# An opening in halves of 256 queries, silu on GpSimd, 14 warm matmuls, and first LayerNorms moved to other steps, in a fused attention and MLP kernel

## The chip, the cores and the metric

The kernel runs on one core of a Trainium2 chip. The metric is the device time in microseconds; quoted times are medians of several executions. Every execution also leaves the span of the core (from the first to the last instruction, some 1.8 us shorter than the time) and the mean clock that the tensor engine was granted. The engines are called PE (tensor engine; PEld is its weight load), DVE (VectorE), ACT (ScalarE), POOL (GpSimd) and SP (SyncE, which issues DMAs).

## The reference

One block of a diffusion transformer: 2048 tokens of width 512, modulated LayerNorm, attention of 32 query heads over 8 cached key/value heads (the last 512 positions), output projection, second modulated LayerNorm, MLP with ReLU.

```python
mod = (_silu(c) @ w_mod).reshape(c.shape[0], 6, 1, -1)
sa, ca, ga, sb, cb, gb = (mod[:, i].copy() for i in range(6))      # shortened
h = _layernorm(x, axis=-1) * (1 + ca) + sa
x = x + ga * _A_ref(h, A_k_cache, A_v_cache, A_wq, A_wo)           # attention, times wo
h = _layernorm(x, axis=-1) * (1 + cb) + sb
x = x + gb * _B_ref(h, B_w1, B_w2)                                 # relu MLP
```

## The kernel before

The queries are worked in 4 blocks of 512; a block has 32 steps, one for each head. In a step PE computes queries for two heads ahead, scores, the product with v, and in most steps four matmuls of the output projection; ACT does the exponentials, DVE divides by the row sum (o). The LayerNorms and modulations are tasks put at chosen steps. First there is an opening, in which the first LayerNorm, the transposes and the modulation of block 0 are done while the weights arrive. `warm(n)` issues n matmuls of 512 columns of ones whose result nobody reads; they are there to get the PE clock up (in the profile of before the first seven start 0.42 us apart, the nine after them 0.22).

```python
    warm(7)
    silu_exp(5)                     # transpose c on PE, exponential on ACT
    warm(9)
    ...                             # statistics of tile 3 on ACT
    ln_stat(0); ln_stat(1); rstd_add(0, 2); rstd_pow(0, 2)      # four lines in the kernel
    ln_stat(2); rstd_add(2, 3); rstd_pow(2, 4)
    silu_mul(5)                     # three small operations on DVE
    for tl in range(3):
        ln_norm(tl)
    ...                             # tile 3 on ACT
    fs = mod_cols_mm(0, QBK)        # 32 matmuls of one column: modulation of block 0
    for f in fs[:len(fs) // 2]:
        f()
    ln_tposes(0, [0, 2])
    for f in fs[len(fs) // 2:]:
        f()
    mod_cols_evac(0, QBK)
    for tl in range(1, TPB):
        ln_tposes(tl, [0, 2])
        warm(tl)
    ln_mod_ps([0, 2], hT[0], R_hT[0], 1)     # hT: two pieces of 512 on DVE, two on ACT
    ...
    q_mms(0)
    q_mms(1, 5)
```

Both LayerNorms of all blocks use one buffer `xn` (normalised) and one `xnT` (its transpose by DMA):

```python
    def ln_dmaT():
        dma(xnT[...], xn[...], "xnT", reads=R_xn, writes=[R_xnT], transpose=True)    # shortened
    ...
    for b in range(1, NB):
        add(H * b - 20, lambda b=b: load_x(b))
        add_ln(b, 1, H * b - 15)             # 11 steps: 4 statistics, rstd, norm, transpose, modulation
    for b in range(NB - 1):
        add_ln(b, 2, H * (b + 1) + 19)
```

So the first LayerNorm of block 2 begins at step 49 and the second of block 0 at step 51.

## Time and profile before

| | before |
|---|---|
| median | 563.0 us of 3 runs; 562.9 of 6 |
| span | 561.0 us |
| PE busy | 550.8 us, 98% |
| first score matmul | 13.40 us |
| step, without and with the output projection | 2.63 and 3.50 us |
| uneven steps | two groups of four, 14.64 and 14.66 us in place of 13.99 |

A kernel whose PE is busy for 98% can only win where PE does nothing that counts. The views that show these places are in the prediction.

### The profile page before, as it was taken

To read this page: it belongs to the slowest core of one execution; us is meant where nothing else is said; L and a number is where in the kernel's file an instruction comes from. 1 tells how busy PE (TensorE), PEld (TensorE's weight loads), DVE (VectorE), ACT (ScalarE), POOL (GpSimd) and SP (SyncE) were. 2 spreads that over 40 slices of the span, in tenths; PEclk is the share of its full clock that TensorE was granted. 3 is DMA by queue.
4 is the path that set the end of the run, shared out by engine and by line. 5 is a ranking of instruction groups with operands and counts; after the bars stand their busy time and mean duration, and the time that the engine had idled before them with its cause. 6 is when DMAs were issued, how large, how long until landed. Compare 5 with 4: busy or idle time off the path is not lost.

```text
span 561.0 us, 9655 instructions
## 1 busy us (share of the span) xinstructions
PE 550.8 (98%) x4057; PEld 314.7 (56%) x4132; DVE 252.4 (45%) x550; ACT 350.4 (62%) x453; POOL 51.7 (9%) x46
## 2 busy tenths in 40 slices
PE   7999999999999999999999999999999999999998
PEld 3565555555555555555555555555555654444444
DVE  3455556643336745333347453333354448321134
ACT  5986666666666666666666666666666644432500
POOL 1020002003220000033000000332000000000000
PEclk9999999999999999999999999999999999999999
DMA  9797566512132155242532531121214210210001
GB/s 270 205 206 176 143 164 88 113 39 38 39 76 39 39 90 136 56 96 57 132 57 57 85 63 39 39 38 39 39 39 72 44 30 0 40 37 23 21 29 47
DMA packets 113308, 42.66 MB, mean 76 GB/s; under 512 B 93928, under 2 KB 112104, under 8 KB 113256
## 3 DMA queue, kind: packets, MB, share of 16 engines
q1 hardware_dynamic: 112024, 40.82, 34.5%
q10 hardware_dynamic: 1232, 1.15, 0.6%
q8 instruction: 33, 0.54, 0.4%
q14 instruction: 19, 0.16, 0.1%
HBM read 18.35 MB, written 2.10 MB: 36 GB/s over the span
## 4 chain that ended last, share of the span: by engine, by line
PE 93%; DMA 4%; DVE 2%; issue 1%; DVEq 0%
PE psS L1367 27%; PE psO L1367 26%; PE psQ L1367 22%; PE psW L1367 18%; DMA xnT<-xn 3%; DMA x<-in_A_x_dram 1%; DVE o L1512 0%; DVE st L1377 0%; DVE xn L1388 0%; PE psS L1370 0%; DVE acc L1534 0%; DVE mv L1378 0%; DVE hT L1396 0%; DVE rinv L1511 0%; DVE rstd L1593 0%
## 5 line engine op out<-in xcount | busy, mean ns | idle before, releaser
L1501 ACT ACTIVATE PT<-psS 128x1024 bf16<-128x1024 f32 x256 | 262.7, 1028 | 128.2 <-PE psS L1367 128.2
L1367 PE MATMUL psS<-qT,kT 128*128 128x512 bf16 x510 | 151.4, 379 | 0.1
L1367 PEld LDWEIGHTS psO<-v,PT 128*128 128x128 bf16 x2048 | 126.3, 98 | 31.9 <-DVE o L1512 2.6
L1367 PE MATMUL psO<-v,PT 128*128 128x129 bf16 x2048 | 137.0, 220 | 0.6 <-DVE o L1512 0.6
L1367 PE MATMUL psQ<-hT,wq 128*128 128x512 bf16 x505 | 130.2, 379 | 0.2
L1367 PE MATMUL psW<-wo,oT 128*128 128x512 bf16 x452 | 118.1, 379 | 3.2
L1511 DVE RECIPROCAL rinv<-psO 128x4 f32<-128x4 f32 x128 | 23.3, 182 | 216.0 <-PE psO L1367 216.0
L1512 DVE TENSOR_TENSOR o<-psO,rinv 128x512 bf16<-128x512 f32 x128 | 88.5, 691 | 4.7 <-DVE rinv L1511 0.3
L1367 PEld LDWEIGHTS psQ<-hT,wq 128*128 128x128 bf16 x508 | 49.6, 98 | 60.7 <-issue 0.5
L1367 PEld LDWEIGHTS psS<-qT,kT 128*128 128x128 bf16 x512 | 49.5, 98 | 58.9 <-ACT PT L1501 0.7
L1493 ACT ACTIVATE qT<-psQ 128x512 bf16<-128x512 f32 x127 | 75.3, 593 | 0.5 <-PE psQ L1367 0.5
L1680 ACT ACTIVATE wq<-psS 128x512 bf16<-128x512 f32 x56 | 33.4, 597 | 49.4 <-PE psS L1367 49.4
L1367 PEld LDWEIGHTS psW<-wo,oT 128*128 128x128 bf16 x512 | 44.9, 98 | 32.9 <-DVE acc L1534 1.2
L1534 DVE TENSOR_TENSOR acc<-psW,acc 128x512 f32<-128x512 f32 x48 | 33.1, 690 | 6.7 <-PE psW L1367 6.7
L1367 PE MATMUL psO<-wmw,wq 128*128 128x512 bf16 (+1 forms) x164 | 32.7, 352 | 0.3
L1537 POOL TENSOR_TENSOR acc<-acc,gaf 128x512 f32<-128x512 f32 x12 | 15.2, 1266 | 156.5 <-DVE acc L1534 149.7
L1383 POOL TENSOR_TENSOR rstd<-rstd,cst 128x4 f32<-128x4 f32 x7 | 7.2, 1033 | 213.5 <-DVE rstd L1382 213.5
L1691 DVE TENSOR_TENSOR PT<-psO,gbf 128x512 f32<-128x512 f32 (+1 forms) x12 | 7.5, 624 | 40.4 <-PE psO L1367 40.4
L1367 PE MATMUL psS<-h2T,wmw 128*128 128x512 bf16 x110 | 25.2, 379 | 0.1
L1367 PEld LDWEIGHTS psO<-wmw,wq 128*128 128x128 bf16 x168 | 15.3, 98 | 16.6
L1367 PE MATMUL psS<-hT,wmw 128*128 128x512 bf16 x110 | 24.4, 379 | 0.1
L1377 DVE BATCH_NORM_STATS2 st<-x 128x6 f32<-128x512 bf16 x31 | 21.0, 678 | 4.7 <-DMA x<-in_A_x_dram 4.7
(77 smaller groups left out, 189.4 us busy)
## 6 DMA issues: line engine op xcount, KB each, us to landing
wo<-in_A_wo_dram SPq DMA_DIRECT2D x4, 1024.0 KB, 6.0
wq<-in_A_wq_dram SPq DMA_DIRECT2D x7, 512.0 KB, 5.7
wmw<-in_B_w_dram SPq DMA_DIRECT2D x14, 256.0 KB, 3.1
wmw<-in_w_mod_dram SPq DMA_DIRECT2D x5, 512.0 KB, 4.8
oT<-o SPq DMA_TRANSPOSE x128, 2.4
out_dram<-PT SPq DMA_DIRECT2D x15, 128.0 KB, 1.7
x<-in_A_x_dram SPq DMA_DIRECT2D x3, 512.0 KB, 4.2
v<-in_A_v_cache_dram SPq DMA_DIRECT2D x8, 128.0 KB, 4.2
```

What stands on the lines that cost most here:

```text
L1367: kb.op(PE, lambda e: e.matmul(out_ap, lhsT, rhs, start=start, stop=stop), reads=reads, group_writes=[R_b[k] for k in bk], signal=signal)
L1377: kb.op(DVE, lambda e: e.bn_stats(st[:, t, :], x_sb[:, t, :]), reads=[R_x[t]], writes=[R_st[t]])
L1383: kb.op(POOL, lambda e: e.tensor_tensor(rstd[:, sl], rstd[:, sl], cst[:, 0:1].to_broadcast([P, hi - lo]), op=ALU.pow), reads=R_rstd[sl] + ...
L1493: kb.op(ACT, lambda e: e.activation(qT[u % NQT][:, :], bank[bk], ACTF.Copy), reads=[R_b[bk]], writes=[R_qT[u % NQT]])
L1501: kb.op(ACT, lambda e: e.activation(PT[u % NPT][:, pr * 2:pr * 2 + 2, :], s_ps[pr][:, :, :], ACTF.Exp, scale=scale), reads=[R_b[pr * 2], R ...
L1511: kb.op(DVE, lambda e: e.reciprocal(rinv[:, u, :], o_ps[:, :, P]), reads=[R_b[5], R_b[6]], writes=[R_rinv])
L1512: kb.op(DVE, lambda e: e.tensor_tensor(o_sb[u % NOS][:, :, :], o_ps[:, :, 0:P], rinv[:, u, :].unsqueeze(2).to_broadcast([P, TPB, P]), op=A ...
L1534: kb.op(DVE, lambda e: e.tensor_tensor(acc[:, tl, :], bank[WBK], acc[:, tl, :], op=ALU.add), reads=[R_b[WBK], R_acc[tl]], writes=[R_acc[tl]])
L1537: kb.op(eng, lambda e: e.tensor_tensor(acc[:, tl, :], acc[:, tl, :], gaf[:, :], op=ALU.mult), reads=[R_acc[tl], R_ga], writes=[R_acc[tl]])
L1680: kb.op(ACT, lambda e: e.activation(h1T[b % 2][:, fc, :], bank[bk], ACTF.Relu), reads=[R_b[bk]], writes=[R_h1[b % 2][fc]], pre=all_events( ...
L1691: kb.op(DVE, lambda e: e.tensor_tensor(yt[i][:, c0:c1], bank[bk][:, c0:c1], gbf[:, c0:c1], op=ALU.mult), reads=[R_b[bk], R_gb], writes=[R_ ...
```

## The change

The intent is to begin the attention sooner and to keep the two LayerNorms of different blocks out of each other's way. Its core (cut):

```diff
-    warm(7)
+    warm(8)
     silu_exp(5)
-    warm(9)
+    warm(5)
...
+    silu_mul()                      # now three operations on POOL, before the statistics
     ln_stat(0)
...
-    silu_mul(5)
...
-    kb.op(ACT, lambda e: e.activation(xn[:, t3, :], ..., ACTF.Identity, scale=rstd..., bias=s3...)
+    kb.op(POOL, lambda e: e.tensor_scalar(xn[:, t3, :], x_sb[:, t3, :], s3..., rstd..., op0=ALU.add, op1=ALU.mult)
...
+    ln_tposes(0, TB[0])
+    ln_tposes(1, TB[0])
+    mod_half(0, 0, DVE)             # 256 columns
+    ln_norm(2)
+    mod_half(0, 2, ACT)
+    mod_half(0, 1, DVE)
+    mod_half(0, 3, ACT)
+    warm(1)
+    q_half(0, 0, CC_ORDER[:2], QBK)
+    ln_tposes(3, TB[1])
+    ln_tposes(2, TB[1])
+    q_half(0, 0, CC_ORDER[2:], QBK)
+    mod_half(1, 0, DVE)
+    mod_half(1, 2, ACT)
+    mod_half(1, 1, DVE)
+    mod_half(1, 3, DVE)
+    q_half(1, 0, CC_ORDER, 5)
+    for u, bk in ((0, QBK), (1, 5)):
+        q_half(u, 1, CC_ORDER, bk)
+        q_evac(u, bk)
...
-        add(H * b - 20, lambda b=b: load_x(b))
-        add_ln(b, 1, H * b - 15)
+        add(H * b - 30, lambda b=b: load_x(b))
+        add_ln(b, 1, H * b - 24)
```

Other small DVE tasks (row maxima of v, parts of the modulation) move to steps that the LayerNorms now leave free.

More of the change, by code (lines that the diff above doesn't have):

```diff
@@ L1258, in build_fast @@
     s3 = T("s3", [P, 4], F32)
+    c_f = T("c_f", [P, DC], F32)
     sc_bf = T("sc_bf", [P, DC])
@@ L1315, in build_fast @@
     R_st, R_mv, R_rstd = RL("st", NT), RL("mv", NT), RL("rstd", NT)
+    R_h0 = RL("h0", DC)
+    R_cf = Res("cf")
     R_s3, R_eps = Res("s3"), Res("eps")
@@ L1401, in ln_tposes @@
         for cc in range(DC):
-            bk = bks[cc // 2]
+            bk = bks[cc]
             o = (cc % 2) * 512 + tl * P
             tpose(bank[bk].bitcast(BF)[:, o:o + P], xn[:, tl, cc * P:(cc + 1) * P], [R_xn[tl]], [bk], cc == DC - 1)
-    def ln_mod_ps(bks, dst, R_dst, which):
-        o, r = (0, R_moda) if which == 1 else (2 * DC, R_modb)
-        for k in range(2):
-            for half, eng in ((0, DVE), (1, ACT)):
-                cc = half * 2 + k
-                src = bank[bks[half]].bitcast(BF)[:, k * 512:(k + 1) * 512]
-                sc, sh = modc[:, o + DC + cc:o + DC + cc + 1], modc[:, o + cc:o + cc + 1]
-                if eng is DVE:
-                    kb.op(DVE, lambda e, src=src, sc=sc, sh=sh, cc=cc: e.tensor_scalar(dst[:, cc, :], src, sc, sh, op0=ALU.mult, op1=ALU.add),
-                          reads=[R_b[bks[half]], r], writes=[R_dst[cc]])
-                else:
-                    kb.op(ACT, lambda e, src=src, sc=sc, sh=sh, cc=cc: e.activation(dst[:, cc, :], src, ACTF.Identity, bias=sh, scale=sc),
-                          reads=[R_b[bks[half]], r], writes=[R_dst[cc]])
     CC_ORDER = (0, 2, 1, 3)
@@ L1426, in silu_exp, with silu_mul @@
         kb.op(ACT, lambda e: e.activation(tmp[:, :], cT, ACTF.Exp, scale=-1.0), reads=[R_b[bk]], writes=[R_tmp])
-    def silu_mul(bk):
-        cT = bank[bk].bitcast(BF)[:, 0:DC]
-        kb.op(DVE, lambda e: e.tensor_scalar(tmp[:, :], tmp[:, :], 1.0, None, op0=ALU.add), reads=[R_tmp], writes=[R_tmp])
-        kb.op(DVE, lambda e: e.reciprocal(tmp[:, :], tmp[:, :]), reads=[R_tmp], writes=[R_tmp])
-        kb.op(DVE, lambda e: e.tensor_tensor(sc_bf[:, :], cT, tmp[:, :], op=ALU.mult), reads=[R_tmp, R_b[bk]], writes=[R_sc])
+        kb.op(ACT, lambda e: e.activation(c_f[:, :], cT, ACTF.Copy), reads=[R_b[bk]], writes=[R_cf])
+    def silu_mul():
+        kb.op(POOL, lambda e: e.tensor_scalar(tmp[:, :], tmp[:, :], 1e38, 1.0, op0=ALU.min, op1=ALU.add), reads=[R_tmp], writes=[R_tmp])
+        kb.op(POOL, lambda e: e.tensor_tensor(tmp[:, :], tmp[:, :], cst[:, 3:4].to_broadcast([P, DC]), op=ALU.pow), reads=[R_tmp, R_eps], writes=[R_tmp])
+        kb.op(POOL, lambda e: e.tensor_tensor(sc_bf[:, :], c_f[:, :], tmp[:, :], op=ALU.mult), reads=[R_tmp, R_cf], writes=[R_sc])
     def mod_cols_mm(which, bk):
@@ L1488, in q_mms, with q_evac @@
         b, h = units[u]
-        order = CC_ORDER if u < QA else range(DC)
-        for i, cc in enumerate(order):
+        for i, cc in enumerate(range(DC)):
             mm(bank[bk], wq_sb[:, cc, h * Dh:(h + 1) * Dh], hT[b % 2][:, cc, :], i == 0, i == DC - 1,
-               [R_wq[h], R_hT[b % 2][cc]], [bk], i == DC - 1)
+               [R_wq[h], R_hT[b % 2][cc]] + ([R_h0[cc]] if b == 0 else []), [bk], i == DC - 1)
+        q_evac(u, bk)
+    def q_evac(u, bk=QBK):
         kb.op(ACT, lambda e: e.activation(qT[u % NQT][:, :], bank[bk], ACTF.Copy), reads=[R_b[bk]], writes=[R_qT[u % NQT]])
@@ L1580, in build_fast @@
     kb.op(POOL, lambda e: e.memset(cst[:, 1:2], eps), writes=[R_eps])
+    kb.op(POOL, lambda e: e.memset(cst[:, 3:4], -1.0), writes=[R_eps])
     kb.op(POOL, lambda e: e.memset(v_sb[:, :, :, P:VW], 1.0), writes=[R_v1])
     kb.op(ACT, lambda e: e.activation(cst[:, 2:3], cst[:, 0:1], ACTF.Exp), reads=[R_cst], writes=[Res("dummy")])
-    warm(7)
+    warm(8)
     silu_exp(5)
-    warm(9)
+    warm(5)
     t3 = TPB - 1
@@ L1605, in build_fast @@
     rstd_pow(2, 4)
-    silu_mul(5)
-    for tl in range(3):
-        ln_norm(tl)
-    kb.op(ACT, lambda e: e.activation(s3[:, 3:4], s3[:, 1:2], ACTF.Copy, scale=rstd[:, t3:t3 + 1]), reads=[R_s3, R_rstd[t3]], writes=[R_s3])
-    kb.op(ACT, lambda e: e.activation(xn[:, t3, :], x_sb[:, t3, :], ACTF.Identity, scale=rstd[:, t3:t3 + 1], bias=s3[:, 3:4]),
-          reads=[R_x[t3], R_rstd[t3], R_s3], writes=[R_xn[t3]])
-    fs = mod_cols_mm(0, QBK)
-    for f in fs[:len(fs) // 2]:
-        f()
-    ln_tposes(0, [0, 2])
@@ L1616, in build_fast @@
-    for f in fs[len(fs) // 2:]:
+    ln_norm(0)
+    ln_norm(1)
+    kb.op(POOL, lambda e: e.tensor_scalar(xn[:, t3, :], x_sb[:, t3, :], s3[:, 1:2], rstd[:, t3:t3 + 1], op0=ALU.add, op1=ALU.mult),
+          reads=[R_x[t3], R_rstd[t3], R_s3], writes=[R_xn[t3]])
+    for f in mod_cols_mm(0, QBK):
         f()
     mod_cols_evac(0, QBK)
-    for tl in range(1, TPB):
-        ln_tposes(tl, [0, 2])
-        warm(tl)
-    ln_mod_ps([0, 2], hT[0], R_hT[0], 1)
+    HB = QB // 2
+    R_half = [R_h0, R_hT[0]]
@@ new lines, in build_fast, with mod_half @@
+    TB = [[0, 0, 2, 2], [1, 1, 3, 6]]
+    def mod_half(hf, cc, eng):
+        bk = TB[hf][cc]
+        o = (cc % 2) * 512 + hf * HB
+        src, dst = bank[bk].bitcast(BF)[:, o:o + HB], hT[0][:, cc, hf * HB:(hf + 1) * HB]
+        sc, sh = modc[:, DC + cc:DC + cc + 1], modc[:, cc:cc + 1]
+        if eng is DVE:
+            kb.op(DVE, lambda e: e.tensor_scalar(dst, src, sc, sh, op0=ALU.mult, op1=ALU.add), reads=[R_b[bk], R_moda], writes=[R_half[hf][cc]])
+        else:
+            kb.op(ACT, lambda e: e.activation(dst, src, ACTF.Identity, bias=sh, scale=sc), reads=[R_b[bk], R_moda], writes=[R_half[hf][cc]])
@@ new lines, in q_half @@
+    def q_half(u, hf, order, bk):
+        for cc in order:
+            mm(bank[bk][:, hf * HB:(hf + 1) * HB], wq_sb[:, cc, u * Dh:(u + 1) * Dh], hT[0][:, cc, hf * HB:(hf + 1) * HB], cc == CC_ORDER[0], cc == CC_ORDER[-1],
+               [R_wq[u], R_half[hf][cc]], [bk], cc == CC_ORDER[-1])
+    ln_tposes(0, TB[0])
[7 more added lines that the diff above has]
+    q_half(0, 0, CC_ORDER[:2], QBK)
@@ L1623, in build_fast @@
+    ln_tposes(3, TB[1])
[8 more added lines that the diff above has]
+        q_half(u, 1, CC_ORDER, bk)
+        q_evac(u, bk)
     load_wq(R, R)
@@ L1625, in build_fast @@
     load_v(1)
-    q_mms(0)
-    q_mms(1, 5)
     kb.op(DVE, lambda e: e.tensor_copy(sc_f[:, :], sc_bf[:, :]), reads=[R_sc], writes=[R_scf])
@@ L1634, in build_fast @@
         for i, op in enumerate((ALU.max, ALU.min)):
-            add(max(R * g, 3), lambda g=g, i=i, op=op: kb.op(DVE, lambda e: e.tensor_reduce(vmax[:, i, g:g + 1], v_sb[:, g, :, 0:Dh], axis=AX.XY, op=op),
+            add((3, 5, 12, 16, 20, 24, 28, 32)[g], lambda g=g, i=i, op=op: kb.op(DVE, lambda e: e.tensor_reduce(vmax[:, i, g:g + 1], v_sb[:, g, :, 0:Dh], axis=AX.XY, op=op),
                                                              reads=[R_v[g]], writes=[R_vmax]))
@@ L1647, in build_fast @@
         add(s, lambda i=i: load_mlp(i))
-    for sl, steps in ((2, (5, 6, 7, 9)), (3, (10, 11, 13, 14)), (4, (15, 25, 26, 27)), (5, (29, 30, 31, 33))):
+    for sl, steps in ((2, (6, 7, 15, 19)), (3, (21, 22, 23, 25)), (4, (26, 27, 29, 30)), (5, (31, 33, 34, 35))):
         for cc, s in enumerate(steps):
             add(s, lambda sl=sl, cc=cc: mod_part(sl, cc))
-    for sl, s in ((2, 10), (3, 27), (4, 38), (5, 105)):
+    for sl, s in ((2, 20), (3, 27), (4, 36), (5, 105)):
         add(s, lambda sl=sl: mod_sum(sl))
```

## The prediction

> **What bounds the kernel now.** I read the page first, then the timeline of the first 18 us, then the gaps between the 128 reciprocals that end the attention steps, then the waits and the chain where those gaps are uneven. The page says that the tensor engine is nearly never idle, at full clock throughout:
>
> ```profile
> PE 550.8 (98%) x4057; PEld 314.7 (56%) x4132; DVE 252.4 (45%) x550; ACT 350.4 (62%) x453; POOL 51.7 (9%) x46
> ...
> PE 93%; DMA 4%; DVE 2%; issue 1%; DVEq 0%
> ```
>
> The reader is to see that there is little to win: only time in which PE runs no useful matmul. There are two such places. The first is the opening, before the first score matmul. The timeline of PE there (start, length, operation, wait before it):
>
> ```profile
> 1.05 3.17 PE L1367 MATMUL psW<-ones 128*128 128x512 bf16 x7 [1.05 <-POOL cst L1577]
> 4.62 0.17 PE L1425 MATMUL psO<-ident,c_row 4*128 4x4 bf16 x1 [0.41 <-DMA c_row<-in_c_dram]
> 4.73 2.13 PE L1367 MATMUL psW<-ones 128*128 128x512 bf16 x9
> 8.18 0.55 PE L1367 MATMUL psQ<-sc_bf,wmw 128*128 128x1 bf16 x16 [1.32 <-DVE sc_bf L1432]
> ...
> 10.53 0.81 PE L1367 MATMUL psW<-ones 128*128 128x512 bf16 x3
> 11.43 1.20 PE L1367 MATMUL psQ<-hT,wq 128*128 128x512 bf16 x4
> 12.46 1.03 PE L1367 MATMUL psO<-hT,wq 128*128 128x512 bf16 x4
> 13.40 0.59 PE L1367 MATMUL psS<-qT,kT 128*128 128x512 bf16 x2
> ```
>
> The work that counts starts at 13.40 us. The second place is the middle. The reciprocals come every 2.63 us in the first steps and every 3.50 us once the wo matmuls run beside attention; the exceptions that cost anything are two groups of four steps, near 205 and 318 us. The same four steps before each group and in it (length; busy time of PE, PEld, DVE, ACT, POOL; clock; DMA share):
>
> ```profile
> 185.99:199.98 13.99, 13.88 (x110) 8.32 (x112) 9.33 (x25) 9.72 (x13) 2.07 (x2) 1.00 0.20 39
> 199.98:214.62 14.64, 14.23 (x110) 8.16 (x112) 7.13 (x18) 9.89 (x13) 0.00 (x0) 1.00 0.75 135
> 298.54:312.53 13.99, 13.88 (x110) 8.33 (x112) 9.32 (x24) 9.72 (x13) 2.02 (x2) 1.00 0.19 39
> 312.53:327.19 14.66, 14.23 (x110) 8.16 (x112) 7.13 (x18) 9.94 (x13) 0.00 (x0) 1.00 0.62 100
> ```
>
> The same 110 matmuls take 0.65 and 0.67 us longer. Why, the waits of 198 to 216 us say (who, for whom; us, times, longest):
>
> ```profile
> DVE xn L1388 <- DMA xnT<-xn: 3.8, 1, 3.8
> DVE hT L1396 <- DMA xnT<-xn: 3.5, 1, 3.5
> PEld psO L1367 <- DVE o L1512: 1.3, 2, 0.8
> ```
>
> Both LayerNorms share xn and xnT. The second one's normalisation may not overwrite xn before the first one's transposing DMA (some 5.9 us in the chain) has read it; DVE stands still in order, the normalisation of o behind it is late, psO is not free, and PE waits. Of two DVE stalls of 3.8 and 3.5 us only 0.65 us reaches PE, because PE has over 2 us of other matmuls between two uses of psO.
>
> [...]four take 1.03 us, which is 3 x 0.216 plus one duration of 0.379. [...]The trace shows [...]seven warm matmuls at (3.17 - 0.63) / 6 = 0.42 us apart, then nine at (2.13 - 0.38) / 8 = 0.22; and that the idle 1.32 us before 8.18 did not bring the slow clock back. No run yet shows what a longer pause does. [...]the trace has 1155 and 1266 ns for its two-input operations of 512 elements, and 740 ns for a power of 2 columns and 1033 ns for one of 4.
>
> **The change, part by part: silu.** It leaves DVE (three operations, 7.55 to 8.12 us) for GpSimd, where the exponential is ready at 5.01. Estimate: add 0.3, power of 4 columns 1.03 (the row of the other such power), multiply 0.3, so sc_bf at about 6.7 instead of 8.12. That is not 1.4 us won: the modulation matmuls also need the first half of w_mod, and its transfer was issued at 1.66:
>
> ```profile
> L1301 SPq DMA_DIRECT2D wmw<-in_w_mod_dram x1: 413/413/413, 1.7 to 1.7; - x1
> ...
> DMA to landing us min/median/max: 6.2/6.2/6.2
> ```
>
> It lands at 1.66 + 6.19 = 7.85. So these matmuls start at about 7.88, not 8.18: 0.30 us won. The first rstd power (6.72 now) should come free about then, so it is delayed by 0.1 at most.
>
> **Order in the opening.** All 32 one-column matmuls now run in one go, 25 ns apart: 7.88 to 8.84. The two evacuations on DVE (0.16 each, spaced as now) give modc at 9.24 (9.75 now). The eight transposes of tiles 0 and 1 follow at 55 ns: last end 9.30.
>
> **Halves.** Before, hT waited for all four tiles, with 5 warm matmuls between them: 10.73. Now the first half starts at about 9.34. A full modulation takes 0.54 on DVE and 0.77 on ACT[...]. DVE: 9.34 to 9.61, norm of tile 2 to 9.95, second piece to 10.13. ACT: to 9.90 and 10.36. On PE the first two half matmuls fit at 9.64 and 9.93; tile 3 (GpSimd's xn: power done at 8.47[...]) is transposed from 10.04 and tile 2 to 10.64. The second half's modulations: DVE 10.68 to 11.35 in three pieces, ACT to 11.24. The last half matmul of unit 0 goes at 11.48 and ends at 11.75. Evacuation 0.60 as now: 12.38. Score matmul, 0.14 later as now: 12.52. **Won: 13.40 - 12.52 = 0.88 us.** wq (9.2), kT (9.7) and v (10.5) land before they are needed. The ramp that follows (evacuation of unit 1, first exponential) has the same gaps as now, so 0.88 carries through: from there on PE is the bound.
>
> **The first LayerNorms** go from 15 to 24 steps before their block, x from 20 to 30. Their transposes and modulations now end at steps 50 and 82; the second LayerNorms start at 51 and 83. The shared buffers meet no more, so both groups should take 13.99: **won 0.65 + 0.67 = 1.32 us.** The third second-LayerNorm, alone today, shows no stall, which supports it. The moved DVE tasks (0.74 or 1.40 us a step) fit in: a step leaves 2.63 - 0.88 = 1.75 us of DVE in the short steps and more later, and the list puts one task in each. Block 1's x (0.5 MB) now loads among w_mod, wo and wq; at some 200 GB/s that delays what is behind it by 2.6 us. wo lands at 31.4 and is used at 38.9, so this is hidden.
>
> **Sum.** 0.88 + 1.32 = 2.2 us; 563.0 - 2.2 = 560.8.
>
> **The rivals.** (1) *The clock falls.* The warm matmuls go from 22 to 14; after the five, PE pauses from about 6.0 to 7.9 and then has only narrow matmuls and transposes until about 10.5. [...]a loss of up to 1.7 us, in all 561.5 to 562.5. Against it: the 1.3 us pause now did nothing[...]. I give it one in eight. (2) *Another wait replaces the one removed.* GpSimd's silu or xn could be slower than I estimate[...]. (3) *The opening gains nothing*, because the landings (x 4.7, w_mod 7.85) fix it: then 561.7. Against: after 7.85 there are 5.5 us of compute, and the halves shorten just that. (4) *The whole of the chain's xnT share returns*: 2.9% of the span, 16 us, which would be 547. Against: PE is busy over nearly all of it; the four-step windows show 0.65.
>
> **Range and chances.** The opening gain may be 0.4 to 1.3, the other 1.1 to 1.4; with a clock that falls at times and 0.3 us of scatter in a median: 560.0 to 561.9. Two per cent would be 11.3 us, and nothing here is that large either way.
>
> **What would show it.** Right: modulation matmuls at 7.9, score matmul near 12.5, 2.63 and 3.50 us steps without exception, no DVE wait on xnT, a span near 558.8. Wrong: a clock under full after 8 us, an idle PE behind GpSimd's xn, or new uneven steps between 8 and 36, where the DVE tasks moved.

The sum was 0.88 + 1.32 = 2.2 us, so 560.8. The ends given for the half pieces imply 0.27 us for one on DVE and 0.56 on ACT: estimates, which the profile of before does not show; `w9_1` has 0.41 and 0.57. The 0.3 each for add and multiply of silu were estimates too (0.28 and 0.20 after). The 200 GB/s are near the 205 and 206 that the page of before gives for 14 to 42 us. The "four" that "take 1.03 us" are matmuls of 512 columns, as at 12.46 us. The "over 2 us" between two uses of psO are 2.43 in the steps before the first group (185.95 to 188.38). In rival (1), for how long the clock stays low was not shown then; the 1.7 us was an estimate (half of the 3.41 us at half clock in the profile after is 1.7).

## More of the kernel before

All executions told of here are of the fast state by time. That label does not separate the clock behaviour of the first 15 us, which turned out to be the subject, so the clock of each execution is given where it matters.

## The result and the profile after

The changed kernel takes **562.34 us** (median of 6, 560.98 to 562.65) against 562.9 for the kernel before (562.78 to 563.45). The ratio is 0.9986, with a 95% interval of 0.9973 to 0.9998. Ratios here are the mean time of one kernel's runs over that of the other's of the same rounds, so not quite the ratio of the medians. Predicted was 560.8, range 560.0 to 561.9. That nothing here would reach two per cent came true, but only 0.6 of the 2.2 us appeared, and the median lies outside the range. The six executions already held the clue:

| time, us | mean granted clock |
|---|---|
| 560.98 | 1.000 |
| 562.02, 562.31, 562.36, 562.61 | 0.997 |
| 562.65 | 0.994 |

The page of the changed kernel, engine shares and chain:

```profile
PE 555.1 (99%) x4132; PEld 316.4 (56%) x4132; DVE 252.9 (45%) x550; ACT 349.5 (62%) x453; POOL 54.5 (10%) x51
...
PE 98%; DMA 1%; DVE 0%; SPq 0%; issue 0%; ACT 0%
```

Of the DMA's 4% of the chain, the 3% that were transposes of xn are gone. PE's longer busy time (555.1 against 550.8) tells nothing: the page of before lacks some matmul records (4057 for 4132 weight loads), this one has all 4132. The steps that were uneven, by the same cut (length; busy time of PE, PEld, DVE, ACT, POOL; clock; DMA share and rate):

```profile
200.91:214.89 13.98, 13.98 (x113) 8.32 (x112) 6.07 (x14) 9.71 (x13) 0.00 (x0) 1.00 0.61 114
312.80:326.79 13.99, 13.99 (x113) 8.32 (x112) 6.08 (x15) 9.72 (x13) 0.00 (x0) 1.00 0.47 76
```

Both groups now take what the others take. (One wait of DVE for xnT is left, 4.2 us near 484 us, after the attention; the kernel before has it too.) In the timeline the first of the 128 row-sum reciprocals comes at 18.07 us before and 18.99 after, the last at 455.70 and 455.30: between them 437.64 and 436.31, so the moved LayerNorms gave **1.33 us** between these two profiles, as predicted (1.32). The opening took 0.93 of it back. The timeline of PE in the opening of the changed kernel (start, length, operation, wait before it):

```profile
1.05 3.59 PE L1370 MATMUL psW<-ones 128*128 128x512 bf16 x8 [1.05 <-POOL cst L1568]
...
4.74 2.23 PE L1370 MATMUL psW<-ones 128*128 128x512 bf16 x5
8.06 0.94 PE L1370 MATMUL psQ<-sc_bf,wmw 128*128 128x1 bf16 x32 [1.08 <-DMA wmw<-in_w_mod_dram]
...
10.06 0.50 PE L1370 MATMUL psQ<-hT,wq 128*128 128x256 bf16 x2 [0.38 <-DVE hT L1616]
10.36 0.53 PE L1373 MATMUL psS<-ident,xn 128*128 128x128 bf16 x3
...
12.49 1.06 PE L1370 MATMUL psQ<-hT,wq 128*128 128x256 bf16 x4
...
14.33 0.59 PE L1370 MATMUL psS<-qT,kT 128*128 128x512 bf16 x2 [0.26 <-ACT qT L1484]
```

The first score matmul comes at 14.33 us, not at 13.40 as before or at 12.52 as predicted. Up to 10.06 things run some 0.4 us behind the plan; after that the matmuls themselves are slow: four of 256 columns take 1.06 us. Three stretches of the same opening, with the granted clock as the third number from the right:

```profile
6.80:10.10 3.30, 1.84 (x43) 1.39 (x42) 2.35 (x9) 0.89 (x3) 2.23 (x4) 1.00 1.26 246
10.20:13.50 3.30, 3.30 (x21) 2.61 (x21) 1.48 (x6) 0.88 (x2) 0.00 (x0) 0.50 1.16 320
13.70:17.00 3.30, 3.04 (x17) 1.16 (x15) 0.00 (x0) 3.05 (x5) 0.00 (x0) 1.00 1.16 312
```

The clock records give the edges: full from 6.76, half from 10.18 to 13.59, full from then on. One window of 3.41 us at half speed, exactly where the queries of the first two heads are computed; a mean clock of 0.997 is that one window (0.5 x 3.41 / 561 = 0.003), 0.994 two, 0.991 three (the profiles of `w5_narrow` and `old_open_14` below, at 0.994 and 0.991, show two and three).

### The profile page after: what moved, and what is told of

Same layout as the page of the kernel before. It is cut to its first block, busy times and chain, and to the rows that moved or that the text cites. A ratio compares the mean times of both kernels' runs of the same rounds, so it can differ in the third digit from the quotient of the medians.

```text
span 560.6 us, 9733 instructions
## 1 busy us (share of the span) xinstructions
PE 555.1 (99%) x4132; PEld 316.4 (56%) x4132; DVE 252.9 (45%) x550; ACT 349.5 (62%) x453; POOL 54.5 (10%) x51
## 4 chain that ended last, share of the span: by engine, by line
PE 98%; DMA 1%; DVE 0%; SPq 0%; issue 0%; ACT 0%
PE psS L1370 28%; PE psO L1370 27%; PE psQ L1370 23%; PE psW L1370 20%; DMA wmw<-in_w_mod_dram 1%; PE psS L1373 0%; SPq L1302 0%; ACT qT L1484 0%; DVE hT L1616 0%; DVE PT L1711 0%; DVE PT L1713 0%; PE psO L1373 0%
## 5 line engine op out<-in xcount | busy, mean ns | idle before, releaser
L1370 PE MATMUL psQ<-hT,wq 128*128 128x512 bf16 (+1 forms) x512 | 131.5, 379 | 0.4 <-DVE hT L1616 0.4
L1370 PE MATMUL psW<-wo,oT 128*128 128x512 bf16 x512 | 130.6, 379 | 0.0
```

The costliest lines, as they stand in the source:

```text
L1370: kb.op(PE, lambda e: e.matmul(out_ap, lhsT, rhs, start=start, stop=stop), reads=reads, group_writes=[R_b[k] for k in bk], signal=signal)
```

## The experiments

**Theory.** With 14 instead of 22 warm matmuls PE does too little in one clock window of the opening, and the next window runs at half speed; the rest of the loss against the prediction is small mis-sizing. **Rivals:** the halves and their waits are slow by themselves or lower the clock by themselves; or the moved tasks cost elsewhere what they gain. The rounds ran on several chips, on which the kernel before had medians from 562.8 to 563.2 us; across rounds the ratios are the fairer comparison.

**1. The LayerNorm part alone** (`ln_only`): the kernel before with the new steps only.

```diff
-        add(H * b - 20, lambda b=b: load_x(b))
-        add_ln(b, 1, H * b - 15)
+        add(H * b - 30, lambda b=b: load_x(b))
+        add_ln(b, 1, H * b - 24)         # and the DVE tasks at the new steps
```

> The kernel before with only the second half of the change: first LayerNorms, x loads and the DVE tasks at their new steps, opening untouched. If the two parts simply add, this gains the 1.32 us that the uneven steps cost: 562.9 - 1.3 = 561.6, granted clock 1.000 in nearly all executions, first score matmul at 13.4 us, no step out of rhythm near 205 and 318 us. If the moved tasks or the earlier x load cost something elsewhere (rival: the missing 1.6 us of the change were lost there), it gains 0.5 us or less and some early step is longer than 2.63 or 3.50 us.

Measured: 562.36 us (561.52, 561.68, 562.36, 562.56, 562.66), ratio 0.9982 (0.9969 to 0.9995). The uneven steps are gone and no other step is out of rhythm (436.31 us from the first to the last reciprocal, as in the change), so nothing is lost there; but only two of five executions show the 561.6 expected. The profiled one took 562.66, and its opening, whose code is untouched, is late:

```profile
1.04 3.17 PE L1367 MATMUL psW<-ones 128*128 128x512 bf16 x7 [1.04 <-POOL cst L1577]
4.86 0.18 PE L1425 MATMUL psO<-ident,c_row 4*128 4x4 bf16 x1 [0.64 <-DMA c_row<-in_c_dram]
4.97 4.02 PE L1367 MATMUL psW<-ones 128*128 128x512 bf16 x9
8.79 0.61 PE L1367 MATMUL psQ<-sc_bf,wmw 128*128 128x1 bf16 x16
```

The nine matmuls take 4.02 us here and took 2.13 in the profile of before: the clock was still half until after 9 us, and the warm matmuls now stand in the way of the modulation. The mean clock says 1.000 all the same: the slow stretch before the first rise is not in the clock records (the answer for 0 to 4 us gives 1.00, where the seven matmuls start 0.42 apart), only the distance of matmuls shows it. So the clock has a second way to cost 0.9 us, a late rise (first score matmul at 14.33 against 13.40).

**2. The opening alone** (`open_only`): the changed kernel with the LayerNorm steps put back (the diff of experiment 1 reversed).

> The changed kernel with the LayerNorm steps put back: the new opening alone. Theory (the new opening lets the clock fall for one 3.4 us window): about 0.7 us slower than before, 563.6, in the executions with clock 0.997, and about 0.9 us faster, 562.0, in those few with clock 1.000; both uneven groups of steps are back. Rival (the new opening is slow for another reason, such as the half-width pieces or GpSimd): slower whatever the clock of the execution is.

Measured: 563.53 us; by clock: 562.82 (1.000), 563.26, 563.53 and 563.68 (0.997), 564.16 (0.994); ratio 1.0009 (0.9996 to 1.0022). The time follows the clock: one half-speed window costs 0.4 to 0.9 us here, two 1.3. That speaks against the rival "slow whatever the clock", on one execution at full clock; and that execution is only level with the kernel before, where I had 562.0: the opening gains less than thought even at full clock.

**3. More warm matmuls** (`more_warm`):

```diff
     silu_exp(5)
-    warm(5)
+    warm(9)
...
-    warm(1)
+    warm(3)
     q_half(0, 0, CC_ORDER[:2], QBK)
```

> The changed kernel with 9 warm matmuls instead of 5 after the transpose of c, and 3 instead of 1 before the first half queries: 20 in place of 14. Theory: the clock stays at 1.000 in most executions and these take about 560.9 (the one execution of the change at full clock took 560.98; up to 0.3 may go into the two added before the half queries). Rival (the clock falls because of the halves and the waits between them, not because of the number of warm matmuls): clock 0.997 as often as with 14, about 562.3.

Measured: **561.41 us** (560.80 to 561.61), clock 1.000 in all five, ratio 0.9968 (0.9955 to 0.9981). Six useless matmuls make the changed kernel 0.9 us faster, though not the 560.9 expected.

**4. Fewer warm matmuls in the old opening** (`old_open_14`): 8, 5 and 1 as in the change, everything else as before.

```diff
-    warm(7)
+    warm(8)
     silu_exp(5)
-    warm(9)
+    warm(5)
...
-        warm(tl)
+        if tl == 2:
+            warm(1)
```

> The kernel before, old opening, with as few warm matmuls as the change has: 8, 5 and 1 in place of 7, 9 and 6; all else as before. Wrong-window theory: the clock falls here too in most executions (0.997 or less), and the time is 1 to 1.7 us longer, 564 or so. Rival (the opening in halves itself lets the clock fall): clock 1.000, and 562.5 to 562.9, as the removed warm matmuls between transposes even save a little.

Measured: 564.69 us (563.47 to 565.25), clock 0.991 in five of six executions and 0.994 in the other; ratio 1.0027 (1.0015 to 1.0039). The profile has three half-speed windows in a row:

```profile
7.70:17.70 10.00, 8.57 (x62) 4.73 (x64) 2.71 (x11) 4.77 (x7) 0.76 (x1) 0.50 1.19 297
```

The old opening falls even deeper with that few. It is the warm matmuls, not the halves.

This run shows something else, which the theory did not ask about. Its LayerNorm steps are the old ones, but its steps are even; the two groups that took 14.64 and 14.66 in the kernel before:

```profile
203.15:217.14 13.99, 13.88 (x111) 8.32 (x112) 7.28 (x19) 9.72 (x13) 0.00 (x0) 1.00 0.73 151
315.04:329.03 13.99, 13.88 (x111) 8.33 (x112) 7.27 (x18) 9.72 (x13) 0.00 (x0) 1.00 0.59 114
```

The first reciprocal comes 3.17 us later than in the profile of before, the last only 1.84. The transposes of xn that the second LayerNorms wait for landed 4.3 us after their issue here, and 5.8 to 5.9 in `before`, `before_8` and `open_only`, where the uneven steps cost 1.2 to 1.3; DVE's wait for xn is 2.3 in place of 3.8, and nothing of it reaches PE. In those three a fetch of instructions (16 KB, DMA queue q8) begins 3.9 to 4.0 us after the issue, before the transpose has landed; here it begins at 4.7, after it. That this fetch is what delays the transpose is likely (the last section has the count over all profiles), but it was not tested.

**5 and 6. Which warm matmuls count?** `w9_1` changes only the 5 to 9, `w5_3` only the 1 to 3.

```diff
-    warm(5)        # w9_1
+    warm(9)
```

```diff
-    warm(1)        # w5_3
+    warm(3)
```

> The changed kernel with only the 5 warm matmuls after the transpose of c made 9 (18 in all). Theory: the window that the clock judged idle in the profile of the change (6.76 to 10.18) then has about one more us of matmuls; clock 1.000 in most executions, 561.2 to 561.4, no slower than with 20. Rival: it is the two added beside the modulations that kept the clock; then 0.997 in most and about 562.3.

> The changed kernel with only the 1 warm matmul before the first half queries made 3 (16 in all). Theory: the idle stretch from 6 or 7 to 8 us stays, so the clock still falls in most executions: 0.997, 562.2 to 562.6. Rival (the added two beside the modulations are what counts): 1.000 and about 561.4.

Measured: `w9_1` **561.44 us** (560.98 to 561.60), clock 1.000 in all five, ratio 0.9968 (0.9955 to 0.9981). `w5_3` 562.43: 561.09 and 561.10 at clock 1.000, 562.30 to 562.78 at 0.997 (three), 563.32 at 0.994; ratio 0.9981. The four in the pause while PE waits for w_mod do it. `w9_1` also shows the new opening at full clock in the profile (PE, as above):

```profile
4.88 3.16 PE L1370 MATMUL psW<-ones 128*128 128x512 bf16 x9
7.93 0.94 PE L1370 MATMUL psQ<-sc_bf,wmw 128*128 128x1 bf16 x32
...
12.03 0.60 PE L1370 MATMUL psO<-hT,wq 128*128 128x256 bf16 x4
12.97 0.59 PE L1370 MATMUL psS<-qT,kT 128*128 128x512 bf16 x2 [0.34 <-ACT qT L1484]
```

Four half-width matmuls take 0.60 here and took 1.06 above. The first score matmul is at 12.97: 0.43 earlier than before, where I had said 0.88.

**7. The late rise** (`ln_8`): the LayerNorm part alone with `warm(8)` instead of `warm(7)`, so that PE does not pause before the transpose of c.

> The LayerNorm part alone with 8 instead of 7 warm matmuls before the transpose of c (nothing else). In the profile of the LayerNorm part alone the clock was still half until some 9 us and the first score matmul came at 14.33 instead of 13.40 us; its five times fall into two groups, 561.5 to 561.7 and 562.4 to 562.7. Theory: the idle 0.4 to 0.6 us between the seventh warm matmul (ends 4.21) and the transpose (4.6 to 4.9) makes a clock window not busy enough, in some executions; the eighth closes it, so all five lie near 561.5, 0.9 us or less apart from none. Rival: the two groups come from the chance position of the window alone; then they stay, about as often.

Measured: **561.52 us** (561.36 to 561.75), all five together; ratio 0.9971 (0.9958 to 0.9983). In five executions the late group did not come back, which supports the theory; five are few to prove that it never does.

**8. The eighth warm matmul in the kernel before** (`before_8`):

```diff
-    warm(7)
+    warm(8)
     silu_exp(5)
```

> The kernel before with 8 instead of 7 warm matmuls before the transpose of c, nothing else. If the idle gap before that transpose only now and then lets the clock rise late, this takes about 562.8 in all five executions, none over 563.1, while the kernel before has some up to 564.2; the LayerNorm part is then worth 562.8 - 561.52 = 1.3 us as predicted. If the eighth warm matmul is itself worth the extra 0.4 us that the LayerNorm part with it gained: 562.4. If it does nothing: as the kernel before in the same rounds, with its tail.

Measured: 562.66 us (562.53 to 563.09), ratio 0.9997 (0.9983 to 1.0011), where the kernel before had 562.47 to 563.68 in the same rounds. Its best executions are no faster, only the slow tail is missing; whether the medians differ is not settled.

**9. Silu back on DVE** (`silu_dve`): experiment 3 with the three operations of silu on DVE after the second power, as before.

```diff
-    silu_mul()
     ln_stat(0)
...
     rstd_pow(2, 4)
+    silu_mul(5)        # add, reciprocal, multiply on DVE
     ln_norm(0)
```

> The kernel with 20 warm matmuls (561.41), with silu put back on the vector engine as it was before. My prediction put the worth of silu on GpSimd at 0.30 us, because the matmuls wait for w_mod until 7.85 anyway. So 561.6 to 561.8 with the modulation matmuls at about 8.2 instead of 8.1. Rival (the move to GpSimd is worth the 1.4 us by which the silu itself is sooner): 562.5 or more. Or it is worth nothing: 561.4.

Measured: 561.45 us (560.85 to 561.88), clock 1.000, against 561.41 (ratios 0.9966 and 0.9968, in different rounds): no difference that can be seen. The modulation matmuls of its profile waited for silu to the last:

```profile
8.30 0.95 PE L1370 MATMUL psQ<-sc_bf,wmw 128*128 128x1 bf16 x32 [1.40 <-DVE sc_bf L1421]
```

w_mod had landed at 8.11 in that execution, late by 0.26. In the changed kernel the same wait ends with the DMA: w_mod lands at 7.92, the matmuls start 0.14 later, at 8.06. By the same 0.14 they could have started at 8.25 here, so silu on DVE (ready at 8.24) cost 0.05. There was little to win: silu on GpSimd is ready sooner, but the transfer lands hardly before silu on DVE would be ready.

**10. Without the halves** (`no_halves`): `w9_1` with all four tiles transposed first and hT modulated in whole pieces of 512, two on DVE and two on ACT; silu and tile 3 stay on GpSimd.

```diff
-    ln_tposes(0, TB[0]) ... mod_half ... q_half ...
+    for tl in (0, 1):
+        ln_tposes(tl, [0, 0, 2, 2])
+    warm(1)
+    for tl in (2, 3):
+        ln_tposes(tl, [0, 0, 2, 2])
+    warm(2)
+    ln_mod_ps([0, 2], hT[0], R_hT[0], 1)
```

> The changed kernel with 9 warm matmuls after the transpose of c (561.44), and the halves undone: the four tiles are normalised and transposed one after the other (with 1 and 2 warm matmuls after them), then modulated over all 512 columns in two pieces on DVE and two on ACT, as before the change, with silu and the fourth tile still on GpSimd. In the profiles a half piece takes 0.41 us on DVE where a whole one takes 0.54, so the seven or eight half pieces cost more than they hide. Theory (the step of my prediction that put a half piece at 0.27 us failed, and the halves are what costs): first score matmul at 12.5 to 12.7 us instead of 12.97, time 561.0 to 561.1. Rival (the halves do gain, and something else held the first score matmul back): 13.4 and 561.8 or more.

Measured: **561.19 us** (560.94 to 561.44), the lowest median of all, a little over the 561.0 to 561.1 expected; ratio 0.9966 (0.9953 to 0.9980), clock 1.000. The profiled execution had w_mod late (8.53), so its 13.45 for the first score matmul says nothing by itself; counted from the first modulation matmul (8.67) it is 4.78 us, against 5.04 in `w9_1` (7.93 to 12.97) and 5.23 in the kernel before (8.18 to 13.40). Other profiles repeat the last two values to 0.01: 5.04 and 5.05 with halves (`more_warm`, `silu_dve`), 5.23 without (`before_8`, `ln_8`). By this count the halves cost 0.26 and do not gain; but 4.78 is one execution, in which the late w_mod left the normalised tiles some 0.3 us more time. In the times the two versions cannot be told apart (0.9966 and 0.9968). Why halves are dear, the pieces of hT show (duration in ns, lowest, median, highest), first before, then `w9_1`:

```profile
L1414 DVE TENSOR_SCALAR hT<-psS,modc x2: 534/539/544, 10.7 to 11.2; 128x512 bf16<-128x512 bf16 x2
```

```profile
L1616 DVE TENSOR_SCALAR hT<-psS,modc x4: 401/407/410, 9.4 to 11.1; 128x256 bf16<-128x256 bf16 x4
```

Half the columns take 76% of the time.

**11. Busy time or columns?** (`w5_narrow`). By then I had counted, from the instruction records, what PE streamed in the clock windows around 4 to 11 us (columns of all matmuls and transposes that start in a window; windows of 3.41 us on the grid of the recorded edges, one execution each):

| window | PE busy, us | columns | next window |
|---|---|---|---|
| after, 6.76 | 1.96 | 2048 | half |
| open_only, 6.09 | 2.15 | 2048 | half |
| old_open_14, 4.18 | 1.66 | 2560 | half |
| w5_3, 6.29 | 2.00 | 2560 | half |
| no_halves, 7.96 | 2.45 | 3072 | full |
| more_warm, 5.43 | 2.57 | 3584 | full |
| silu_dve, 4.89 | 2.01 | 4096 | full |
| before, 4.22 | 2.24 | 4608 | full |
| before, 7.63 | 2.82 | 4608 | full |

(The 32 single-column matmuls of the modulation add at most 32.) Busy time does not sort them: 2.15 fell and 2.01 stayed. Nor does the longest pause: the clock fell after windows with 1.08 to 1.41 us (after, `w5_3`) and stayed after one with 1.40 (`silu_dve`). Columns do, if transposes are counted: without them the window of `no_halves`, which stayed, has 1024, and that of `old_open_14`, which fell, 2560. The test keeps PE as busy, with next to no columns:

```diff
     warm(5)
+    for i in range(32):
+        mm(bank[WBK][:, 0:1], ones[:, :], ones[:, 0:1], True, True, [R_ones], [WBK], i == 31)
```

> The changed kernel with 32 matmuls of one column each (25 ns apart, some 0.9 us) after the 5 warm ones: PE as busy in time as with the 9 warm matmuls that kept the clock, but with 32 columns streamed in place of 2048. If what the clock judges is columns streamed in a 3.41 us window (in the profiles so far it fell after windows with 2048 to 2560 columns and stayed after windows with 3072 and more), it falls as often as in the change: 0.997 in most executions, about 562.3. If it judges busy time, or the idle gap itself, the clock stays: 1.000 and about 561.4.

Measured: 562.34 us; 560.86 (1.000), 561.99, 562.30 and 562.38 (0.997), 562.74 and 562.95 (0.994); ratio 0.9984 (0.9972 to 0.9997). It falls like the change. In its profile the window from 4.39 to 7.81 has 2592 columns, and the clock is half for two windows after it (4.45 to 7.75, then 7.90 to 14.60):

```profile
4.45:7.75 3.30, 2.28 (x39) 1.45 (x38) 2.83 (x9) 2.16 (x8) 2.20 (x5) 1.00 1.06 356
7.90:14.60 6.70, 5.97 (x64) 4.84 (x65) 2.96 (x11) 2.08 (x4) 1.45 (x2) 0.50 1.21 291
```

With PE busy for 2.28 of 3.30 us and no pause above 0.91 us in the window, the clock still fell. Busy time does not decide here; columns streamed fit all ten windows (the nine and this one), with an edge between 2592 and 3072 of some 8,100 that full speed could stream (an estimate: 3.413 us at the 0.216 us per 512 columns of the 40 matmuls from 521.40 us in the profile after, (8.80 - 0.38) / 39). That is an inference from ten windows at full speed, not a measured rule. Windows at half speed, which the table leaves out, do not give quite the same edge: by the same count the clock stayed at half after 1920 and 3200 columns (`old_open_14`, 7.59 and 11.01 us) and 2048 (`w5_narrow`, 7.81), and rose after 3584 and more. The 3200 lie above the 3072 that kept the full speed. A second edge for the rise would fit, and so would the error of the count, since a matmul of 512 columns that straddles a window's end is counted whole.

## Why the prediction was wrong

**The LayerNorm step held.** "both groups should take 13.99": 13.98 and 13.99 measured; "won 0.65 + 0.67 = 1.32 us": 1.33. That 3.8 and 3.5 us of DVE stall were worth only 0.65 us also held, and so did the point that the DMA's 16 us of the chain would not come back. The earlier x load and the moved tasks cost nothing: no uneven steps, in any of the nine kernels with the new steps. What the prediction took as given is the length of the transpose, 5.9 us: with 4.3, in the profile of `old_open_14`, the old steps are even too and there is nothing to win. So 1.33 is what the move gives where the transpose is slow, as in the three other profiles with the old steps.

**The step that failed is rival (1), "The clock falls ... I give it one in eight".** The fall and its size were named (561.5 to 562.5 in all), but it was weighed as the exception, and it is the usual case: five of six executions. The argument that failed was "the 1.3 us pause now did nothing": that pause did nothing while nine wide matmuls lay in the same window (4608 columns); in the window before the fall 1.96 of 3.42 us were busy, with 2048 columns. Experiments 3, 4, 5 and 11 show it from both sides: put the warm matmuls back and the clock stays in ten of ten executions; take them from the old opening and it falls in six of six.

**Of "Won: 13.40 - 12.52 = 0.88 us", 0.43 was there at full clock** (12.97 in the profile of `w9_1`). The term that was mis-sized is the half piece on DVE, put at 0.27 ("9.34 to 9.61"): 0.41 measured, because only 0.13 of a whole piece's 0.54 goes with 256 columns (0.5 ns each), where the estimate took off 0.27. The last of the second half's three pieces ended 1.05 us after the first began (10.80 to 11.85 in `w9_1`), where I had 0.67 (10.68 to 11.35). Next, "7.85 ... start at about 7.88": a matmul that waited for that DMA started 0.14 after its landing (7.92 to 8.06 in the change, 8.53 to 8.67 in `no_halves`). So of "0.30 us won" by silu 0.2 was there in the profile of before (8.18 against 7.85 + 0.14), 0.05 in that of `silu_dve`, and nothing visible in the times (experiment 9), though the reason given, that the transfer of w_mod is the bound, is right. GpSimd kept to the plan: silu done at 6.81 (6.7 said), xn 8.65 to 9.42 (needed at 10.04 by the forecast); rival (2) did not occur.

**Even the 0.43 is not seen in the times.** `w9_1`, with the new opening, and `ln_8`, with the old one, both with the LayerNorm part and full clock, take 561.44 and 561.52. What stays open: how much of the profile's gain is eaten by the varying landing of w_mod (7.79 to 8.53 in these profiles), which differs between executions by as much as the gain. Open too is why the four executions with 14 to 16 warm matmuls and the new steps that kept the full clock (560.86 to 561.10) lie below the medians with 18 and 20 (561.44 and 561.41): no profile shows one of them, and the only such execution of `open_only` gained nothing.

**The sum, then:** 1.33 from the LayerNorms; 0.0 to 0.4 from the opening at full clock (some 0.6 in the best execution of the change, 562.9 - 560.98 - 1.33); and 1.0 to 1.7 lost in the change and in `w5_3` to half-speed windows (560.98 against 562.02 to 562.65; 561.1 against 562.30 to 562.78), 2.2 in the worst execution; most executions have one such window. The range ended at 561.9, between the rare case of a full clock and the usual one.

A version that beats both is four wide matmuls away from the change (`w9_1`, 561.44), or the LayerNorm part alone with one more than before (`ln_8`, 561.52); the lowest is the new opening without its halves (`no_halves`, 561.19). Among these three the times do not decide.

## What to carry to other kernels

Warm matmuls in a wait of PE cost nothing here as long as they ended before it did (in `more_warm` PE still waited 0.84 us for w_mod after them, at 561.41 against 562.34 us; in `ln_only` the nine took 4.02 us and the modulation began at 8.79 in place of 8.18), and they are not spare: before removing any, count the columns in each 3.4 us of the opening, which sorted the windows here, and look at the clock of several executions, not of one profile. Cutting an operation in two is only worth it where its time goes with its length (half the columns took 407 of 539 ns on DVE here); take the fixed part from two rows of different length before counting on half. When two users of one buffer collide, read the price from the length of the steps (0.65 us here), not from the length of the wait (3.8), and in more than one profile (with the transpose at 4.3 us in place of 5.9, nothing reached PE).

## What else the profiles show

- The clock records have two values only, 1.00 and 0.50; the stretch at 0.50 in the opening is 3.41 us long (after), or two or three times that (`w5_narrow`, `old_open_14`), at a position that changes from execution to execution (first rise between 4.18 and 7.02 us in the records). In the change the longest gap in the window before the fall was 1.08 us and PE was busy for 1.96 of its 3.42 us, and the clock was halved for the next 3.41 us; in `w5_narrow` 32 one-column matmuls (0.8 us of busy PE) did not help.
- The mean granted clock of a run can read 1.000 although the first rise came late (`ln_only`: 4.02 us for nine matmuls, 562.66 against 561.5 us).
- In a modulation from psS on DVE 256 columns more cost 132 ns (539 - 407), and the fixed part of a duration is some 275 ns (407 - 132). Two pieces in a row start 0.32 us apart, so some 0.19 of it recurs.
- On GpSimd a power took 0.70 to 0.82 us for two columns and 1.03 to 1.05 for four. A one-input tensor-scalar operation of 512 elements with two scalar operands took 0.77 us in most profiles (0.82 in `silu_dve`, 0.90 in `no_halves`).
- Of the 91 transposes of xn in the 13 profiles, 62 landed 4.2 to 4.5 us after their issue and 29 after 5.3 to 6.2; in all 29 a fetch of instructions began 0.8 to 4.3 us after the issue, in the others only at the last transpose of each profile (near 480 us) and at two more. That the fetch is the cause was not tested.
